# Three buffers for the first weights, the fourth one lent to a weight conversion, and one raw load per group moved forward

## The chip, the cores and the metric

The kernel runs on one core of a Trainium2 chip. The metric is the time of one execution on the device, in microseconds (us). TensorE (PE) multiplies matrices from SBUF into PSUM; VectorE (DVE) and ScalarE (ACT) work element by element; GpSimd (POOL) here does little but issue adding transfers; SyncE (SP) does nothing but issue the other transfers, one after the other: a transfer that has to wait for something holds up those behind it.

## The reference, cut to what matters

Windowed attention gives `x` (1152 tokens of 512), which goes through a mixture of four experts and then through one layer with a rational function:

```python
p = domain_probs / (domain_probs.sum(-1, keepdims=True) + 1e-09)
for e in range(E):                       # 4 experts, w1[e] 512x1024, w2[e] 1024x512
    h = np.maximum(x @ w1[e], 0.0)
    out += p[:, e:e + 1] * (h @ w2[e])
...
h = x @ w_in                             # 512x2048, given in float64
g = (a[0] + a[1]*h + a[2]*h*h + a[3]*h*h*h) / (1 + |b[0]|*|h| + |b[1]|*h*h + 1e-6)
return (g @ w_out).astype(np.float32)    # 2048x512, given in float64
```

## The kernel before, in words

**Split operands.** Every operand of a large product is kept as two parts: a rounded high part (made by an ACT copy) and the rest (made by a DVE subtraction). A product is three multiplications: high by high, high by low, low by high.

**Stages.** First comes attention, with the first group's products between its steps. Then come the groups of the expert layer. The expert layer's 4096 hidden columns are cut into 16 units `u` of 256, two to a group `g` (0 to 7), so there are 16 tiles `w1[u]` and 16 tiles `w2[u]`. The last stage treats the rational layer's 2048 columns as units 16 to 23, in an order written out by hand (`DENSE`).

**A group, g = 2 to 6.** On PE it has two plain first products (`h_paced`, L452: `ps_h<-xh,w`) for a third of the tokens, two calls of `strassen` (L904 and on), which make the other two thirds with seven products of blocks and of sums of blocks (L920: `ps_h<-...`), and nine second products (`o_paced`, L497: `ps_o<-w,hh` and `ps_o<-w,hl`). Inside `strassen` two DVE additions stand between PE's own products: PE cannot begin the next product before ACT has copied the fifth product to `p5` (L942) and DVE has added it (L943), and again later (L927). `relu_parts` makes the hidden operand's parts from a finished product: `hh` on ACT (L469), `hl` on DVE (L473). A second product needs both.

**Raw weights.** `load_w1` and `load_w2` (L139) load a unit's float32 tile (512 KB) into one of four `raw` buffers. `split_later` then copies it to the high half of a `w` tile (ACT, L815) and subtracts for the low half (DVE, L819). A `w1` tile also gets its block sums (L157) and those are split to `sw` (L840, L845). There are four `w` tiles of 8 KB a partition for `w1` and four for `w2`.

**The conversion.** While the groups run, `convert` turns the rational layer's float64 weights into float32 parts and stores them in DRAM. It works on half tiles: a load `x64` (L220, 512 KB, two buffers), some DVE steps (L242, L252, L269, L273, L283, L296) and one on ACT (L255) that give `f`, an ACT copy `high_part` (L225) and a DVE subtraction `low_part` (L229) into **one** split buffer `w` of 4 KB a partition, and a store of that buffer to DRAM (L230, 512 KB). The next `high_part` must wait until that store has landed. For six units (18 to 23) it also makes block sums in a buffer `sums` taken from the four `raw` ones, copies their high part into the same split buffer (L279), stores it (L280), subtracts (L286) and stores `sums` (L287).

**What sets the order.** `Pace` lays the steps of DVE and ACT between PE's products by a table of costs (`COST`), so the order on each engine is fixed when the program is built. `Window.open` says when the conversion may begin a unit with sums, and `Window.loaded` with the test `late` puts off the copy of the sums when raw loads have just been issued. `weights_free` runs when the first sums of a group are split, and issues the group's raw loads: `w1[u+3]`, `w2[u+2]`, `w2[u+3]`. The last one waits (`Window.waiting`) until the sums in work are stored.

Of the kernel before, what the change touches and what calls it, by code (L numbers as in the profile page):

```python
# [94 lines left out]
"""  # L95
COST = dict(h=2.09, p=1.045, o=2.74, osum=0.78, relu=1.0, add=0.59, split=0.67, sums=0.42, bits=0.41, both=1.15, token=1.0)
QSCALE = 1.0 / D ** 0.5
# [4 lines left out]
def body(ctx, tc, qkv, mask, dp, w1, w2, w1d, w2d, coef, out):  # L102
# [4 lines left out]
    hp = ctx.enter_context(tc.tile_pool(name="hp", bufs=6))  # L107
    wp = ctx.enter_context(tc.tile_pool(name="wp", bufs=4))
    dram = ctx.enter_context(tc.tile_pool(name="dram", bufs=1, space=DRAM))
    rawp = ctx.enter_context(tc.tile_pool(name="rawp", bufs=4))  # L110
# [20 lines left out]
    w1s, w2s, scratch = {}, {}, {}  # L131

    def load_w(src, store, nm):
        def load(u, halves=(slice(0, 1024),)):
            if u < 2 * NG1:
                if halves[0].start == 0:
                    store[u] = rawp.tile([128, 1024], F32, tag="raw", name="raw")
                for s in halves:
                    nc.sync.dma_start(store[u][:, s], src[u][:, s])  # L139
            elif u < 2 * NG:  # L140
                store[u] = wp.tile([128, 2, 1024], F32R, tag=nm, name=nm)
                nc.sync.dma_start(store[u].bitcast(F32), scratch[nm, u])
        return load
# [16 lines left out]
    def split_w(store, nm):  # L160
        def split(u, halves=(0, 1)):
            if u >= 2 * NG1:
                return
            if halves[0] == 0:
                raws[nm, u] = store[u]
                store[u] = wp.tile([128, 2, 1024], F32R, tag=nm, name=nm)
            raw, w = raws[nm, u], store[u]
            for i in halves:
                s = slice(i * 512, (i + 1) * 512)

                early = nm == "w1" and u < 2
                (nc.vector.tensor_copy if early else nc.scalar.copy)(w[:, 0, s], raw[:, s])
                nc.vector.tensor_tensor(
                    out=w[:, 1, s], in0=raw[:, s], in1=w[:, 0, s].bitcast(F32), op=ALU.subtract
                )
        return split
# [12 lines left out]
    class Window:  # L189

        open, loaded = False, -99.0
        waiting = []

    def convert(pool):
# [8 lines left out]
        def begin():  # L203
# [17 lines left out]
            return (nm, u, i), s, x, whole  # L221

        def high_part(f):
            w = pool.tile([128, 2, 512], F32R, tag="w", name="w")
            nc.scalar.copy(w[:, 0], f)  # L225
            return w
# [8 lines left out]
        while nxt or done:  # L235
# [29 lines left out]
            if x is not None:  # L265
# [9 lines left out]
                )  # L275
            late = x is None or Pace.pe - Window.loaded > 6.0
            if whole is not None and late:
                ws = pool.tile([128, 2, 512], F32R, tag="w", name="w").rearrange("p a b -> p (a b)")
                nc.scalar.copy(ws, whole)  # L279
                nc.sync.dma_start(scratch["sw", u][:, 0], ws.bitcast(F32))  # L280
            if x is not None:
                yield COST["split"]
                nc.vector.tensor_tensor(out=f, in0=f, in1=t.bitcast(F32), op=ALU.add)  # L283
            if whole is not None and late:
                yield COST["both"]
# [321 lines left out]
    with tc.manual_schedule():  # L607
# [53 lines left out]
        def split_high(n, u, i):  # L661
            store, nm = raw_of[n][1], f"w{n}"
            if i == 0:
                raws[nm, u] = store[u]
                store[u] = wp.tile([128, 2, 1024], F32R, tag=nm, name=nm)
            s = slice(i * 512, (i + 1) * 512)
            nc.scalar.copy(store[u][:, 0, s], raws[nm, u][:, s])
# [135 lines left out]
        def split_later(store, nm, u, wait=0.0):  # L803
            opens = nm == "w2" and u % 2 == 0

            def new(i):
                if i == 0:
                    raws[nm, u] = store[u]
                    store[u] = wp.tile([128, 2, 1024], F32R, tag=nm, name=nm)
            for i in range(2):  # L810
# [12 lines left out]
                def last(low=low):  # L823
                    low()
                    Window.open = True
                behind(0.0, (nm, u), act_then((nm, u), act, last if opens and i else low, COST["split"]), wait)

# [142 lines left out]
        def weights_free(*us):  # L970
            Window.open, Window.loaded = False, Pace.pe
            loads(*us)

        for g in range(NG1):
# [19 lines left out]
            if g in BLOCKED:  # L994
# [15 lines left out]
                w2_loads = (load_w2, u + 2), (load_w2, u + 3)  # L1010
                free = [(weights_free, *([(load_w1, u + 3)] if g > 1 else []), *(w2_loads if again else ()))]
                fills[2].insert(0, (sums_split_later, u + 1, 0, free))
# [6 lines left out]
                else:  # L1019
                    loads((load_w1, u + 4))  # L1020
                strassen(u + 1, (o((g, 0)), o((g, 1)), o((g, 2) if again else (g - 1, 8))))
                if again:
                    sums_split_later(u + 2, 0, [(loads, (load_w1, u + 4))])
                    sums_later(u + 3)
                else:
                    loads(*w2_loads, (load_w1, u + 5))

# [265 lines left out]
```

## Time and profile before

| what | value |
|---|---|
| three runs | 635.31, 637.47, 637.83 us; median 637.47 us |
| the profiled execution | 638.02 us, of which the span of the profile is 636.2 us |
| PE busy | 624.5 us (98%), 3726 matmuls |
| weight loads on PE | 556.7 us (88%) |
| DVE busy | 522.4 us (82%) |
| ACT busy | 369.2 us (58%) |
| POOL busy | 87.7 us (14%) |
| transfers | 111.28 MB, mean 175 GB/s |

The profiled execution is 0.55 us above the median and 1.8 us above its own span (what lies before the first and behind the last instruction). A wait is listed as the engine and line that waited, what ended the wait, the total, the times and the longest. The chain of waits follows the work that ended last back from the end. In the timeline the idle time ahead of an instruction stands in brackets. Names stand without their numbers: `x` is `x64`, `p` is `p5`, and `w<-w` is a store of a split buffer or a load of stored weights. SPq is SyncE issuing a transfer; a row of its timeline begins when it issues, not when the data has landed.

### The profile page before, as it was taken

How to read it: one execution, taken by the hardware profiler on the slowest of the kernel's cores; microseconds unless marked ns; L12 is line 12 of the kernel's file. 1: busy time of each engine (PE TensorE's matmuls, PEld its weight loads, DVE VectorE, ACT ScalarE, POOL GpSimd, SP SyncE). 2: the span in 40 equal slices, each digit the busy share in tenths (PEclk: the TensorE clock that was granted, in tenths of full speed). 3: DMA queues.
4: the chain of work that ended last, by engine and by line, in shares of the span. 5: the costliest groups of instructions: out<-in, count | busy, mean ns of one | idle time of the engine just before them, and what ended most of it. 6: DMA issues, size and time to landing. Idle time of an engine off the chain costs nothing.

```text
span 636.2 us, 9843 instructions
## 1 busy us (share of the span) xinstructions
PE 624.5 (98%) x3726; PEld 556.7 (88%) x3728; DVE 522.4 (82%) x788; ACT 369.2 (58%) x682; POOL 87.7 (14%) x103
## 2 busy tenths in 40 slices
PE   8999999999999999999999989999999999999997
PEld 4888898988989989899999978988998889899886
DVE  7687488889888888888879688438898899899994
ACT  6787624354554655454554454227688687877760
POOL 2223330011111111112111201000000002111110
PEclk9999999999999999999999989999999999999999
DMA  9955302259889778959778967870331563572333
GB/s 277 316 157 167 116 1 67 100 163 247 225 239 248 225 210 251 276 168 254 222 205 231 270 194 194 262 267 8 125 133 36 184 211 94 116 239 50 67 80 102
DMA packets 39535, 111.28 MB, mean 175 GB/s; under 512 B 4256, under 2 KB 5024, under 8 KB 37440
## 3 DMA queue, kind: packets, MB, share of 16 engines
q1 hardware_dynamic: 29264, 92.41, 43.6%
q0 software_dynamic: 9936, 18.09, 16.4%
q8 instruction: 29, 0.48, 0.3%
q10 hardware_dynamic: 288, 0.16, 0.1%
q14 instruction: 18, 0.15, 0.1%
HBM read 67.13 MB, written 25.43 MB: 145 GB/s over the span
## 4 chain that ended last, share of the span: by engine, by line
PE 91%; DMA 4%; DVE 3%; ACT 1%; issue 0%; POOL 0%; ACTq 0%; POOLq 0%
PE ps_o L497 42%; PE ps_h L452 21%; PE ps_h L920 14%; PE ps_h L1149 7%; DMA w<-w 3%; PE ps_v L416 2%; PE ps_s L402 1%; DMA raw<-in_w_dram 1%; PE ps_h L497 1%; PE ps_s L347 1%; PE ps_h L639 1%; PE ps_h L1083 1%; DVE hl L473 0%; DVE w L229 0%; DVE w L819 0%
## 5 line engine op out<-in xcount | busy, mean ns | idle before, releaser
L497 PE MATMUL ps_o<-w,hh 128*128 128x512 f32 (+1 forms) x848 | 229.6, 392 | 1.3 <-ACT hh L469 1.0
L497 PEld LDWEIGHTS ps_o<-w,hh 128*128 128x128 f32 x848 | 156.5, 188 | 29.7 <-ACT hh L469 1.5
L452 PE MATMUL ps_h<-xh,w 128*128 128x384 f32 x512 | 138.8, 339 | 0.0
L497 PE MATMUL ps_o<-w,hl 128*128 128x512 f32 (+1 forms) x424 | 132.0, 393 | 1.8 <-DVE hl L473 1.7
L497 PEld LDWEIGHTS ps_o<-w,hl 128*128 128x128 f32 x424 | 79.4, 188 | 20.0 <-DVE hl L473 2.7
L452 PEld LDWEIGHTS ps_h<-xh,w 128*128 128x128 f32 x512 | 93.9, 189 | 1.7 <-issue 0.3
L452 PE MATMUL ps_h<-xl,w 128*128 128x384 f32 x256 | 86.1, 336 | 0.0
L528 POOL DMA_DIRECT2D acc<-part x51 | 44.6, 875 | 282.0 <-ACT part L527 225.9
L527 ACT ACTIVATE part<-ps_o,p_sb 128x512 f32<-128x512 f32 x51 | 35.0, 686 | 59.1 <-PE ps_o L497 40.7
L469 ACT ACTIVATE hh<-ps_h 128x768 fp32r<-128x768 f32 x48 | 37.4, 810 | 31.3 <-PE ps_h L452 21.1
L473 DVE SCALAR_TENSOR_TENSOR hl<-ps_h,hh 128x768 fp32r<-128x768 f32 x48 | 44.5, 951 | 9.6 <-ACT hh L469 9.4
L452 PEld LDWEIGHTS ps_h<-xl,w 128*128 128x128 f32 x256 | 48.4, 189 | 0.8
L1068 POOL DMA_DIRECT2D acc<-part x18 | 15.6, 867 | 184.3 <-ACT part L1067 183.8
L920 PE MATMUL ps_h<-t,sw 128*128 128x384 f32 x168 | 34.4, 340 | 1.4 <-DVE ps_h L943 1.4
L819 DVE TENSOR_TENSOR w<-raw,w 128x512 fp32r<-128x512 f32 x48 | 32.9, 685 | 1.6 <-ACT w L815 1.5
L920 PEld LDWEIGHTS ps_h<-t,sw 128*128 128x128 f32 x168 | 30.2, 188 | 3.9 <-DVE ps_h L943 1.8
L381 ACT ACTIVATE pr<-pr,mx 128x80 f32<-128x80 f32 (+1 forms) x84 | 29.8, 358 | 6.1 <-DVE mx L375 4.7
L920 PE MATMUL ps_h<-xh,sw 128*128 128x384 f32 x112 | 33.2, 337 | 0.0
L920 PE MATMUL ps_h<-xh,w 128*128 128x384 f32 x112 | 33.1, 335 | 0.0
L564 DVE SCALAR_TENSOR_TENSOR sq<-sq,absb,ab 128x768 f32<-128x768 f32 x24 | 24.3, 1014 | 8.0 <-ACT sq L553 6.7
L815 ACT CAST w<-raw 128x512 fp32r<-128x512 f32 x48 | 28.1, 616 | 4.1 <-DMA raw<-in_w_dram 4.1
L255 ACT ACTIVATE x<-x 128x512 f32<-128x512 f32 x32 | 21.8, 681 | 13.7 <-DVE t L252 9.1
(133 smaller groups left out, 1082.7 us busy)
## 6 DMA issues: line engine op xcount, KB each, us to landing
acc<-part POOLq DMA_DIRECT2D x69, 256.0 KB, 3.9
raw<-in_w_dram SPq DMA_DIRECT2D x32, 512.0 KB, 6.1
w<-w SPq DMA_DIRECT2D x32, 512.0 KB, 3.7
w<-w SPq DMA_DIRECT2D x16, 1024.0 KB, 6.0
x<-in_w1d_dram SPq DMA_DIRECT2D x16, 512.0 KB, 4.2
x<-in_w2d_dram SPq DMA_DIRECT2D x16, 512.0 KB, 4.9
sw<-sw SPq DMA_DIRECT2D x12, 512.0 KB, 7.2
sw<-w SPq DMA_DIRECT2D x6, 512.0 KB, 2.7
```

The lines of the kernel that those rows point to most:

```text
L381: nc.scalar.activation(pr[:, j, i], pr[:, j, i], AF.Exp, scale=-1.0, bias=self.mx[:, j, i:i + 1], accum_out=self.total[:, j, i:i + 1],)
L452: nc.tensor.matmul(ps[:, i, :TC], lhsT=a[:, k, f], rhs=b[:, k], start=k + n == 0, stop=k + n == 5,)
L469: nc.scalar.activation(new_h(u, c)[0], ps[:, :, :TC], AF.Relu)
L473: nc.vector.scalar_tensor_tensor(out=hl, in0=ps[:, :, :TC], scalar=0.0, in1=hh.bitcast(F32), op0=ALU.max, op1=ALU.subtract,)
L497: nc.tensor.matmul(ps, lhsT=a[:, i, tk], rhs=b[:, i, cols], start=v + n == 0, stop=v + n == 6)
L527: nc.scalar.activation(part, ps, AF.Copy, scale=pe)
L528: nc.gpsimd.dma_start(acc[t], part, accum_op=ALU.add)
L564: nc.vector.scalar_tensor_tensor(out=self.sq, in0=self.sq, scalar=absb[:, 1:2], in1=self.ab, op0=ALU.mult, op1=ALU.add,)
L815: nc.scalar.copy(store[u][:, 0, s_], raws[nm, u][:, s_])
L819: nc.vector.tensor_tensor(out=w[:, 1, s_], in0=raws[nm, u][:, s_], in1=w[:, 0, s_].bitcast(F32), op=ALU.subtract)
L920: nc.tensor.matmul(out, lhsT=a[i][:, k], rhs=b[j][:, k], start=first and k + n == 0, stop=k + n == 3, skip_group_check=not first,)
L1149: nc.tensor.matmul(out, lhsT=a[i][:, k], rhs=b[j][:, k], start=first and k + m == 0, stop=k + m == 3, skip_group_check=not first,)
```

## The change

1. `w1` gets three buffers in place of four. A new single tile `lone` of the same size stands in for the fourth: it holds `w1[3]` early on, and `w1[19]` and `w1[23]` at the end (`weight_tile`).
2. Between those uses the two halves of `lone` are lent to the conversion as two more split buffers. `split_buffer` takes the pool's own buffer, `lone[:, 0]` and `lone[:, 1]` in turn, for `high_part` and for the copy of the sums.
3. One raw load per group moves forward: `w2[u+2]` is issued when the second half of the odd `w2` tile before it has been split (early in the group), not with the other raw loads in `weights_free`.
4. The test `late` and `Window.loaded` go: the copy of the sums is made as soon as the sums are there.
5. In the last group `w1[17]`, `w1[18]` and `w1[19]` are loaded one step later each.
6. `COST["split"]` goes from 0.67 to 0.68, so that the table lays DVE's and ACT's steps a little differently.

```diff
-COST = dict(..., split=0.67, ...)
+COST = dict(..., split=0.68, ...)
...
+    lone = ctx.enter_context(tc.tile_pool(name="lone", bufs=1)).tile([128, 2, 1024], F32R, name="lone")
...
+    def weight_tile(nm, u):
+
+        if nm == "w1" and (u == 3 or u >= 2 * NG1 and u % 4 == 3):
+            return lone
+        return wp.tile([128, 2, 1024], F32R, tag=nm, name=nm, bufs=3 if nm == "w1" else 4)
...
-                store[u] = wp.tile([128, 2, 1024], F32R, tag=nm, name=nm)
+                store[u] = weight_tile(nm, u)
...
+        def split_buffer():
+            Window.spare.append(Window.spare.pop(0) if Window.spare else None)
+            own = pool.tile([128, 1024], F32R, tag="w", name="w") if Window.spare[-1] is None else None
+            return own if own is not None else Window.spare[-1]
+
         def high_part(f):
-            w = pool.tile([128, 2, 512], F32R, tag="w", name="w")
+            w = split_buffer().rearrange("p (i n) -> p i n", i=2)
             nc.scalar.copy(w[:, 0], f)
             return w
...
-            late = x is None or Pace.pe - Window.loaded > 6.0
-            if whole is not None and late:
-                ws = pool.tile([128, 2, 512], F32R, tag="w", name="w").rearrange("p a b -> p (a b)")
+            if whole is not None:
+                ws = split_buffer()
                 nc.scalar.copy(ws, whole)
                 nc.sync.dma_start(scratch["sw", u][:, 0], ws.bitcast(F32))
...
                 def last(low=low):
                     low()
-                    Window.open = True
+                    if u % 2 == 0:
+                        Window.open = True
+                    elif u + 1 < 2 * NG1:
+                        load_w2(u + 1)
...
                 w2_loads = (load_w2, u + 2), (load_w2, u + 3)
-                free = [(weights_free, *([(load_w1, u + 3)] if g > 1 else []), *(w2_loads if again else ()))]
+                free = [(load_w1, u + 3)] * (g > 1) + [w2_loads[0]] * (g == 1) + [w2_loads[1]]
+                free = [(weights_free, *free)] if again else []
...
-                    loads((load_w1, u + 4))
+                    loads((load_w1, u + 3))
                 strassen(u + 1, (o((g, 0)), o((g, 1)), o((g, 2) if again else (g - 1, 8))))
+                if g == 1:
+                    Window.spare[:] = [None, lone[:, 0], lone[:, 1]]
...
-                    loads(*w2_loads, (load_w1, u + 5))
+                    loads(*w2_loads, (load_w1, u + 4), (load_w1, u + 5))
```

**The order on PE** is the same in both programs, row by row, apart from the name of the tile. The order of DVE, ACT and SP changes from the second group on. Line numbers of the changed file are 10 to 16 higher (L139 becomes L146, L220 L228, L230 L243, L287 L299, L819 L829, L943 L956).

SP's queue in group 4 before, from the store of the sums of unit 20 on. `raw_2790` is `w1[11]`, `raw_2792` and `raw_2794` are `w2[10]` and `w2[11]`, `x64` are loads of the conversion:

```order
L280 DMA sw_20_1394<-w_2772 128x1024
L287 DMA sw_20_1394<-sums_2486 128x1024
L139 DMA raw_2790<-in_w1_dram 128x1024
L139 DMA raw_2792<-in_w2_dram 128x1024
L139 DMA raw_2794<-in_w2_dram 128x1024
L220 DMA x64_2803<-in_w2d_dram 128x1024
L230 DMA w2_18_1380<-w_2821 256x1x512
```

The same place now, with what stands ahead of it; `raw_2635` is `w2[10]`, `raw_2769` `w1[11]`, `raw_2806` `w2[11]`:

```order
L146 DMA raw_2635<-in_w2_dram 128x1024
L243 DMA w2_18_1383<-lone_73 256x1x512
L228 DMA x64_2677<-in_w2d_dram 128x1024
L243 DMA w1_20_1391<-lone_73 256x1x512
L228 DMA x64_2721<-in_w2d_dram 128x1024
L243 DMA w1_20_1391<-w_2734 256x1x512
L146 DMA raw_2769<-in_w1_dram 128x1024
L292 DMA sw_20_1397<-lone_73 128x1024
L299 DMA sw_20_1397<-sums_2507 128x1024
L146 DMA raw_2806<-in_w2_dram 128x1024
L228 DMA x64_2840<-in_w2d_dram 128x1024
L243 DMA w2_18_1383<-lone_73 256x1x512
```

The load of `w2[10]` moved ahead of three stores, two `x64` loads, the load of `w1[11]` and both stores of the sums. The load of `w2[11]` still stands right behind the store of the sums, and it takes the buffer that this store frees, in groups 3 to 6 alike. Three buffers take turns where one did.

SP's queue in group 6 before (`raw_3687` is `w1[15]`, `raw_3689` and `raw_3709` are `w2[14]` and `w2[15]`):

```order
L280 DMA sw_22_1396<-w_3683 128x1024
L139 DMA raw_3687<-in_w1_dram 128x1024
L139 DMA raw_3689<-in_w2_dram 128x1024
L287 DMA sw_22_1396<-sums_3402 128x1024
L139 DMA raw_3709<-in_w2_dram 128x1024
L220 DMA x64_3712<-in_w2d_dram 128x1024
L230 DMA w2_22_1384<-w_3767 256x1x512
```

And now (`raw_3670` is `w1[15]`, `raw_3672` `w2[15]`; `w2[14]` is loaded five rows ahead of this piece):

```order
L292 DMA sw_22_1399<-lone_73 128x1024
L299 DMA sw_22_1399<-sums_3356 128x1024
L146 DMA raw_3670<-in_w1_dram 128x1024
L146 DMA raw_3672<-in_w2_dram 128x1024
L228 DMA x64_3681<-in_w2d_dram 128x1024
L243 DMA w2_21_1386<-lone_73 256x1x512
```

Two raw loads stood between the two stores of the sums; none does now.

DVE's queue in group 3 of the changed kernel. The row ahead of these, `L308 ... f_2277<-x64_2192`, frees the buffer into which `x64_2332` is loaded; that load stands on SP behind the store of the sums and two raw loads, as above:

```order
L255 TENSOR_SCALAR t_2334<-x64_2242 128x512
L265 SCALAR_TENSOR_TENSOR t_2334<-x64_2242,t_2334 128x512
L242 TENSOR_TENSOR lone_73<-f_2277,lone_73 128x512
L282 TENSOR_SCALAR f_2347<-t_2334 128x512
L164 TENSOR_TENSOR raw_2081<-raw_2081 128x2x128
L485 SCALAR_TENSOR_TENSOR hl_2349<-ps_h_2201,hh_2348 128x768
L485 SCALAR_TENSOR_TENSOR hl_2352<-ps_h_2202,hh_2351 128x768
L164 TENSOR_TENSOR raw_2081<-raw_2081 128x2x128 x3
L286 SCALAR_TENSOR_TENSOR f_2347<-x64_2242,f_2347 128x512
L295 TENSOR_TENSOR f_2347<-f_2347,t_2334 128x512
L858 TENSOR_TENSOR sw_2392<-raw_2081,sw_2392 128x512
L956 TENSOR_TENSOR ps_h_2355<-ps_h_2354,p5_2402 128x384
```

Behind them come `L308 ... f_2347<-x64_2242` and `L829 ... w2_2418`, and then `L255 ... t_2424<-x64_2332`, the first use of the new load. That is 16 instructions between the two uses of the buffer; in groups 4, 5 and 6 it is 14, 18 and 18.

## Rows read from the trace of the kernel before

**Rows 1.** The page's first part: busy time, share of the span, instructions.
```profile
PE 624.5 (98%) x3726; PEld 556.7 (88%) x3728; DVE 522.4 (82%) x788; ACT 369.2 (58%) x682; POOL 87.7 (14%) x103
```
**Rows 2.** Table by stretches: length, five engines' busy time, PEclk, DMA share, GB/s.
```profile
182.86:230.76 47.90, 47.90 (x242) 43.35 (x241) 42.50 (x75) 25.20 (x42) 7.80 (x9) 1.00 0.82 235
230.76:280.32 49.56, 48.16 (x241) 43.27 (x241) 42.77 (x74) 26.30 (x44) 7.86 (x9) 1.00 0.81 230
```
**Rows 3.** Waits of PE from 78 to 430 us, the longest three.
```profile
PE ps_o L497 <- DVE hl L473: 1.7, 1, 1.7
PE ps_h L920 <- DVE ps_h L943: 1.4, 1, 1.4
PE ps_o L497 <- ACT hh L469: 1.0, 1, 1.0
```
**Rows 4.** The chain of waits from 228 to 264 us: start, length, what.
```profile
227.98 2.77 PE ps_h L452 x16
...
239.59 4.48 DMA w<-w
...
245.52 3.65 DMA w<-w
...
252.53 7.76 DMA raw<-in_w_dram
...
261.35 0.58 DVE ps_h L943
```
**Rows 5.** PE's timeline from 355 to 392 us, at the longest wait.
```profile
374.46 1.22 PE L497 MATMUL ps_o<-w,hl 128*128 128x512 f32 x2 [1.69 <-DVE hl L473]
```
**Rows 6.** Table by stretches again: the four microseconds behind that wait.
```profile
374.00:378.00 4.00, 3.54 (x12) 3.35 (x13) 3.93 (x9) 1.71 (x3) 0.56 (x1) 0.57 0.55 195
```
**Rows 7.** SP's timeline from 345 to 372 us: start of issue, length, line.
```profile
348.92 0.33 SPq L280 DMA_DIRECT2D sw<-w  x1
349.29 1.26 SPq L139 DMA_DIRECT2D raw<-in_w_dram  x2
350.65 0.41 SPq L287 DMA_DIRECT2D sw<-sums  x1
358.89 0.33 SPq L139 DMA_DIRECT2D raw<-in_w_dram  x1
359.31 0.41 SPq L220 DMA_DIRECT2D x<-in_w2d_dram  x1
359.81 1.08 SPq L230 DMA_DIRECT2D w<-w  x1
```
**Rows 8.** DVE's timeline from 361 to 376 us.
```profile
366.18 0.43 DVE L242 TENSOR_SCALAR t<-x 128x512 uint32<-128x512 uint32 x1 [4.25 <-DMA x<-in_w2d_dram]
...
369.59 0.69 DVE L229 TENSOR_TENSOR w<-f,w 128x512 fp32r<-128x512 f32 x1 [1.79 <-ACT w L225]
...
372.59 1.81 DVE L473 SCALAR_TENSOR_TENSOR hl<-ps_h,hh 128x768 fp32r<-128x768 f32 x2
...
374.92 1.34 DVE L157 TENSOR_TENSOR raw<-raw 128x256 f32<-128x256 f32 x3
```
**Rows 9.** The chain of waits from 355 to 386 us, at the same place.
```profile
359.81 9.03 DMA w<-w
```
**Rows 10.** Waits of ACT from 86.86 to 410 us, one of them.
```profile
ACT w L225 <- DMA w<-w: 20.1, 8, 5.3
```
**Rows 11.** Transfers of one line to landing: line 287 (`sums` stores).
```profile
DMA to landing us min/median/max: 3.2/3.5/8.2
```
**Rows 12.** The same for line 220 (`x64` loads).
```profile
DMA to landing us min/median/max: 3.2/4.4/9.6
```
**Rows 13.** The page's part 6: transfers by line, count, KB, median us to landing.
```profile
raw<-in_w_dram SPq DMA_DIRECT2D x32, 512.0 KB, 6.1
w<-w SPq DMA_DIRECT2D x32, 512.0 KB, 3.7
w<-w SPq DMA_DIRECT2D x16, 1024.0 KB, 6.0
```

More of the change, by code (lines that the diff above doesn't have):

```diff
@@ L95 @@
 """
-COST = dict(h=2.09, p=1.045, o=2.74, osum=0.78, relu=1.0, add=0.59, split=0.67, sums=0.42, bits=0.41, both=1.15, token=1.0)
+COST = dict(h=2.09, p=1.045, o=2.74, osum=0.78, relu=1.0, add=0.59, split=0.68, sums=0.42, bits=0.41, both=1.15, token=1.0)
 QSCALE = 1.0 / D ** 0.5
@@ L165, in split @@
                 raws[nm, u] = store[u]
-                store[u] = wp.tile([128, 2, 1024], F32R, tag=nm, name=nm)
+                store[u] = weight_tile(nm, u)
             raw, w = raws[nm, u], store[u]
@@ L189, in body @@
     class Window:
-        open, loaded = False, -99.0
+        open = False
         waiting = []
+        spare = []
     def convert(pool):
@@ L283, in convert @@
                 nc.vector.tensor_tensor(out=f, in0=f, in1=t.bitcast(F32), op=ALU.add)
-            if whole is not None and late:
+            if whole is not None:
                 yield COST["both"]
@@ L664, in split_high @@
                 raws[nm, u] = store[u]
-                store[u] = wp.tile([128, 2, 1024], F32R, tag=nm, name=nm)
+                store[u] = weight_tile(nm, u)
             s = slice(i * 512, (i + 1) * 512)
@@ L803, in split_later @@
         def split_later(store, nm, u, wait=0.0):
-            opens = nm == "w2" and u % 2 == 0
             def new(i):
@@ L808, in new @@
                     raws[nm, u] = store[u]
-                    store[u] = wp.tile([128, 2, 1024], F32R, tag=nm, name=nm)
+                    store[u] = weight_tile(nm, u)
             for i in range(2):
@@ L824, in last @@
                     low()
-                    Window.open = True
-                behind(0.0, (nm, u), act_then((nm, u), act, last if opens and i else low, COST["split"]), wait)
+                    if u % 2 == 0:
+                        Window.open = True
+                    elif u + 1 < 2 * NG1:
+                        load_w2(u + 1)
+                behind(0.0, (nm, u), act_then((nm, u), act, last if nm == "w2" and i else low, COST["split"]), wait)
         sw = {}
@@ L970, in weights_free @@
         def weights_free(*us):
-            Window.open, Window.loaded = False, Pace.pe
+            Window.open = False
             loads(*us)
```

## The prediction

> **What bounds the kernel now.** The page's first part comes first: PE is busy 98% of the span, DVE 82%, ACT 58% [rows 1]. So PE's own work is the floor, and only what lets PE stand still or run slowly can be won. PE's order and work do not change, so the next question is where PE loses time in the stretch that the change touches, the groups from 87 to 430 us.
>
> The table by stretches answers it. An undisturbed group lasts 47.90 us and PE is busy for all of it. The next one lasts 49.56 us [rows 2]: 1.66 us lost. PE's waits name the places: 1.4 us for the DVE addition L943, which is the loss in that group, and 1.0 us for `hh` and 1.7 us for `hl` right after each other [rows 3], at 371 to 374 us [rows 5]. Behind this last pair the granted clock falls: over 374 to 378 us it is 0.57 of full speed [rows 6], so part of that stretch ran at 1.2 GHz instead of 2.4. That costs 4 x (1 - 0.57) = 1.72 us more. In all
>
> 1.66 + 1.0 + 1.7 + 1.72 = 6.1 us, 1.0% of the span.
>
> This is the most the change can win in the groups.
>
> Why PE waited is read from the chain of waits. Ahead of the first loss it goes twice through the store of the split buffer, 4.48 and 3.65 us, then through the load of a raw weight tile, 7.76 us, and ends in L943 [rows 4]. DVE ran late because ACT could not refill the only split buffer; being late, it freed a raw buffer late; the raw load that waited for it came late; and ACT, which works in order, stood before the `w2` copy with the copy to `p5` behind it.
>
> Ahead of the second loss SP's queue was held. It issued two raw loads and the store of the sums at 349 to 351 us, and then nothing until 358.89, because the next raw load needed the buffer that this store frees [rows 7]: 8.24 us. The conversion's load and its store, queued behind, went out at 359.31 and 359.81. DVE waited 4.25 us for that load and 1.79 us for ACT, 6.0 us together [rows 8], and ACT was waiting for the store, which took 9.03 us to land [rows 9]. DVE's `hl` came at 372.6 [rows 8], and PE stood.
>
> **The change part by part.**
>
> *Two more split buffers.* Waits of ACT for the one buffer sum to 20.1 us in eight places, up to 5.3 us [rows 10]. With three buffers in turn a refill needs the store of three uses earlier. A half tile takes DVE seven operations (L242, L252, L269, L273, L283, L296, L229) of 0.43 to 0.69 us [rows 8], some 4 us, so three uses lie about 12 us apart. A store lands in 3.7 us in the median [rows 13] and took 9.03 at its worst place [rows 9]. So these waits go. Nothing replaces them on DVE: the number of operations is the same. The gain on PE is between 0 (all cover elsewhere) and 6.1 us.
>
> *The raw load moved forward.* In group 4 `w2[u+2]` was issued at 252.53 us and landed 7.76 us later, with the path to L943 waiting for it [rows 4]. Three stores and two `x64` loads of the conversion lie between its new place and the old, three half tiles at some 4 us, so it goes out about 12 us earlier or more. That is seven times the 1.66 us by which it was late; this closes the first loss even where a store is slow. What it passes are stores and `x64` loads: each stands behind 512 KB more for one transfer's time. Between nothing and 3 us per passed transfer (9.03 us for the last of three issued together, [rows 7, 9]), and covered because the loads it passes are used many operations later. I take 0.
>
> *The load of `w2[u+3]`* stays right behind the store of the sums and still waits for its landing, so SP is still held once in each of groups 3 to 6. What changes is how long. In group 6 two raw loads and a store were queued ahead of the store of the sums, and it took 8.24 us; in the changed order only the other store of the sums is, or one raw load more in group 4. The median landing is 3.5 us, the worst 8.2 [rows 11]. Group 3 is tightest: between freeing the `x64` buffer and its next use stand 16 operations. By the rows: 1.81 us for the two `hl`, 1.34 and a third of it for the four raw sums, two narrow ones at 0.43, seven at up to 0.69 [rows 8] and the addition at 0.58 [rows 4], 9.9 us. The store of the sums goes out about 1.4 us (two operations) before the buffer is free; SP is held to 3.5 - 1.4 = 2.1 us after; the load then lands 4.4 us later in the median, 9.0 behind two raw loads [rows 12, 9]. So 6.5 to 11.1 us against 9.9: DVE waits 0 to 1.2 us. Since 6.0 us of such waits gave PE 2.7 us of waiting [rows 8, 3], the first 3.3 us reach nobody. I take 0; the upper end, with a store of 8.2 us, is a rival below.
>
> By the Trainium skill, "DMA: Bandwidth & Descriptors", section "Queues, rings and completion order", each DMA engine consumes the descriptors of a ring in order. By that rule a load that is pulled forward delays what stands behind it by its full length, the store of the sums and `x64` too, and the sum would be that of the slower rival below. The trace agrees where three transfers went out together in group 6: the third landed last. It does not agree that this is the usual case: the median `x64` load lands in half of that time.
>
> *Three `w1` buffers.* A new `w1` tile now waits for the unit three before instead of four. ACT's copy for `w1[u+3]` stands behind the `hh` copies that wait for the last product of `strassen(u)`, the same product that frees the buffer. It waits for nothing new. If that cover went, it would be one product of six matmuls, 2.77 x 6/16 = 1.04 us [rows 4].
>
> *The last loads.* `w1[18]` and `w1[19]` go out behind `w2[16]` and `w2[17]`. 1 MB takes 6.0 us [rows 13]; four of them 24 us. The first product with `w1[18]` stands behind twelve bank steps of twelve matmuls in `DENSE`, 12 x 12 x 2.77/16 = 25 us by the same row, and behind the second products between them. 0.
>
> *Dropping `late`, 0.68 for 0.67.* These shift the order by an operation or two; the additions that PE waits for keep their place between the same products. I put 0.5 us on this and on all else that is new, between 0 and the 1.66 us of one loss like the first.
>
> **The sum** against the profiled execution: 638.02 - 6.1 + 0.5 = 632.4 us. That execution is 0.55 us above the median of the runs, so against the median: 637.47 - 5.6 = **631.9 us**.
>
> **The rivals.** What a measurement of this kernel can tell from no change is 0.5%, 3.2 us: below 634.3 is faster, above 640.7 slower.
>
> *One loss stays.* For: the losses come once in some six groups, so small shifts make and unmake them. If one like the first stays: 631.9 + 1.66 = 633.6, still faster. If one like the second stays, clock and all (2.7 + 1.72 = 4.4): 636.3, no change. The second is for the reader who distrusts the step on SP: the queue is held as before, only behind fewer bytes.
>
> *The buffers are not what binds.* ACT works in order, and its split copies often stand behind a copy that waits for PE. Then DVE's wait for ACT stays with any number of buffers: 637.5. Against it: the waits of ACT at L225 name the store [rows 10].
>
> *SP's hold becomes the bound: slower.* The store of the sums lands late (8.2 us) in each group, since the pulled-forward load and the undelayed copy of the sums bunch the transfers; `x64` comes 4.7 us later than above, 11.2 to 15.8 us after its buffer is free. DVE then waits up to 5.9 us in group 3. It decides from 3.3 us of DVE waiting in a group; each group beyond that costs what the second loss cost, 4.4 us. Three groups: 637.47 - 6.1 + 3 x 4.4 = 644.6 us. Two give 640.2, which is no change yet. Against it: half of the six stores of sums landed in 3.5 us or less [rows 11], and groups 5 and 6 have 18 operations for cover. (The Trainium skill's rule on ring order, above, is this rival's.)
>
> **How the numbers follow.** Both losses go: 0.70 (631.9). One like the first stays: 0.08 (633.6). One like the second stays: 0.10 (636.3). The buffers do not bind: 0.07 (637.5). SP's hold: 0.05 (644.6). Faster 0.70 + 0.08 = 0.78, no change 0.17, slower 0.05. The range goes from 630.0, the forecast less its 0.5 and less 1.4 for runs that spread from 635.31 to 637.83, to 636.5, which takes in one loss like the second and leaves out 0.12 and a little of the rest.
>
> **What would show it.** Right: no wait of PE over 0.3 us from 130 to 415 us, granted clock 1.00 all through, every group 47.9 us; ACT's waits for stores at the split copies near 0; SP still held for about 3 us once in groups 3 to 6. A step is wrong if DVE waits for `x64` for over 3.3 us in a group, if ACT still waits for a store of a split buffer, or if PE waits at L956 (the old L943). The forecast is wrong if PE's waits in the groups sum to over 2 us or if the clock falls once.

## The result, and the profile after

The changed kernel takes **631.46 us** in the median of 6 runs (631.32 to 632.67), the kernel before 637.60 us in the median of 6 (635.31 to 640.90). The ratio is 0.9908, with a 95% interval from 0.9880 to 0.9936: faster by about 0.9%. Forecast were 631.9 us and a range from 630.0 to 636.5. The runs also lie closer together: 1.35 us from lowest to highest, against 5.6 us.

The page's first part of the changed kernel answers to [rows 1]; PE is now busy 99% of a span of 629.6 us (before: 636.2).

```profile
PE 622.5 (99%) x3726; PEld 556.3 (88%) x3728; DVE 522.9 (83%) x788; ACT 370.2 (59%) x682; POOL 87.7 (14%) x103
```

These are all waits of PE that the whole span holds (total, times, longest). The three of [rows 3] are gone, and none of these four lies in the groups: they are two places at PE's start, one of the attention and one second product at 77.7 us, ahead of the stretch that the change touches.

```profile
PE ps_h L651 <- DVE warm L641: 1.2, 1, 1.2
PE ps_s L414 <- POOL pr L403: 0.7, 1, 0.7
PE ps_h L651 <- issue: 0.3, 1, 0.3
PE ps_o L509 <- DVE xl L452: 0.3, 1, 0.3
```

The table by stretches answers to [rows 2, 6]: every group from 135 us on lasts 47.90 us, PE is busy for all of each, and the granted clock is 1.00.

```profile
182.86:230.76 47.90, 47.90 (x242) 43.38 (x241) 41.15 (x71) 25.17 (x43) 7.81 (x9) 1.00 0.81 227
230.76:278.65 47.89, 47.89 (x242) 43.36 (x241) 42.54 (x74) 25.10 (x43) 7.82 (x9) 1.00 0.84 232
326.55:374.44 47.89, 47.89 (x242) 43.36 (x241) 40.56 (x70) 25.43 (x43) 7.82 (x9) 1.00 0.85 238
374.44:414.00 39.56, 39.56 (x200) 35.21 (x199) 27.55 (x45) 15.65 (x25) 4.43 (x5) 1.00 0.75 229
```

In the table of ACT's waits the row of 20.1 us for the split buffer's store [rows 10] has no successor. What the split copies (L238, L291) still wait for is DVE. The only wait for a transfer is the one for `acc`, in two places.

```profile
ACT lone L291 <- DVE sums L164: 2.8, 2, 2.3
ACT w L238 <- DVE f L308: 2.0, 1, 2.0
...
ACT part L539 <- DMA acc<-part: 4.7, 2, 3.2
```

SP is still held behind each store of the sums: 3.5 us in group 3, 5.5 in group 4, where one raw load more goes out ahead of the two stores, 3.2 in group 5 and 3.3 in group 6. Its timeline in group 6 answers to [rows 7]: the store is issued at 346.03 and the load that it holds at 349.32 us, 3.3 us later in place of 8.24. (The row of two raw loads spans the hold: the second waits.)

```profile
342.33 0.33 SPq L292 DMA_DIRECT2D sw<-lone  x1
346.03 0.33 SPq L299 DMA_DIRECT2D sw<-sums  x1
346.63 3.02 SPq L146 DMA_DIRECT2D raw<-in_w_dram  x2
349.75 0.46 SPq L228 DMA_DIRECT2D x<-in_w2d_dram  x1
```

The tightest place is in group 3. There the `x64` load went out at 205.06 us, and DVE waited 0.55 us for it, as DVE's timeline shows (the one wait of this kind before was 4.25 us, ahead of group 7, [rows 8]):

```profile
212.44 0.43 DVE L255 TENSOR_SCALAR t<-x 128x512 uint32<-128x512 uint32 x1 [0.55 <-DMA x<-in_w2d_dram]
```

So the time went where the forecast looked for it. By PE's timeline the same second products begin 0.33 us earlier than before in group 3 (182.37 for 182.70), 2.01 us earlier in group 5 (278.15 for 280.16) and 6.64 us earlier in group 7 (373.94 for 380.58), and that lead stays to the end. So the first loss gave back 1.7 us and the second 4.6, its waits and the low clock together. The other 0.3 us lie at the start, in a stretch that the change does not touch.

### The profile page after: what moved, and what is told of

The parts are those of the page before. It is cut to its first block, busy times and chain, and to the rows that moved or that the text cites. A ratio compares the mean times of both kernels' runs of the same rounds, so it can differ in the third digit from the quotient of the medians.

```text
span 629.6 us, 9848 instructions
## 1 busy us (share of the span) xinstructions
PE 622.5 (99%) x3726; PEld 556.3 (88%) x3728; DVE 522.9 (83%) x788; ACT 370.2 (59%) x682; POOL 87.7 (14%) x103
## 4 chain that ended last, share of the span: by engine, by line
PE 97%; DVE 1%; ACT 0%; POOL 0%; issue 0%; POOLq 0%
PE ps_o L509 46%; PE ps_h L464 21%; PE ps_h L933 16%; PE ps_h L1165 7%; PE ps_v L428 2%; PE ps_s L414 1%; PE ps_h L509 1%; PE ps_s L359 1%; PE ps_h L651 1%; PE ps_h L1099 1%; DVE mx L387 0%; DVE pr L377 0%; POOL pr L403 0%; PE ps L359 0%; DVE xl L889 0%; DVE hl L485 0%
## 5 line engine op out<-in xcount | busy, mean ns | idle before, releaser
L464 PE MATMUL ps_h<-xh,w 128*128 128x384 f32 x464 | 125.3, 338 | 0.0
L464 PEld LDWEIGHTS ps_h<-xh,w 128*128 128x128 f32 x464 | 84.4, 188 | 1.3
L464 PE MATMUL ps_h<-xl,w 128*128 128x384 f32 x232 | 77.7, 335 | 0.0
L464 PEld LDWEIGHTS ps_h<-xl,w 128*128 128x128 f32 x232 | 43.6, 188 | 0.6
L829 DVE TENSOR_TENSOR w<-raw,w 128x512 fp32r<-128x512 f32 x48 | 32.8, 684 | 1.0 <-ACT w L825 0.9
L933 PE MATMUL ps_h<-xh,w 128*128 128x384 f32 x104 | 30.7, 336 | 0.0
L825 ACT CAST w<-raw 128x512 fp32r<-128x512 f32 x48 | 27.9, 616 | 0.0
```

Source lines behind the costliest of these rows:

```text
L464: nc.tensor.matmul(ps[:, i, :TC], lhsT=a[:, k, f], rhs=b[:, k], start=k + n == 0, stop=k + n == 5,)
L825: nc.scalar.copy(store[u][:, 0, s_], raws[nm, u][:, s_])
L829: nc.vector.tensor_tensor(out=w[:, 1, s_], in0=raws[nm, u][:, s_], in1=w[:, 0, s_].bitcast(F32), op=ALU.subtract)
L933: nc.tensor.matmul(out, lhsT=a[i][:, k], rhs=b[j][:, k], start=first and k + n == 0, stop=k + n == 3, skip_group_check=not first,)
```

## The experiments

The question is which part of the change did it. The forecast gave the second loss (4.4 us) to the two further split buffers and the first (1.66 us) to the moved raw load, and it held the shift of the order for nothing. All kernels below were timed in 5 rounds, in three sets on three chips, each ratio against runs of the kernel before on the same chip. Those had medians of 638.81 us (11 runs) beside the kernel with one buffer, the two with the raw load put back and the one with the buffers in the old order; 638.65 us (17 runs) beside the one with two buffers and the three with the raw load, the price or `late` changed alone; and 638.61 us (29 runs, 634.71 to 641.27) beside the four on the hold of SP, the third set. Line numbers differ by a few from kernel to kernel.

**One part taken from the change.** First the two further split buffers:

```diff
-                if g == 1:
-                    Window.spare[:] = [None, lone[:, 0], lone[:, 1]]
```

> The changed kernel with one split buffer instead of three (the lent fourth weight buffer stands idle); order of every engine and the moved raw load as changed. Theory (one buffer makes DVE late): ACT's waits for stores of the split buffer come back, 15 to 25 us in sum in the groups, some half tile ends late enough for PE, and one loss like the second of before returns: 633.0 to 637.5 us, PE waits of 1 to 3 us in the groups and a stretch with the clock below 1.00. Rival A (the moved raw load and the new order did it): ACT's waits come back but no PE wait over 0.5 us, 631.0 to 632.3 us.

Measured: 633.37 us (632.70 to 634.58), ratio to before 0.9913 [0.9886, 0.9940]. The theory holds in its time, at the lower end, and in the kind of wait: some 1.9 us come back, not 6. ACT waits for the stores again, 27.9 us in two rows (15 to 25 were expected). PE has one loss, like the first of before but at another place, 197.95 us, and the low clock that was expected does not come:

```profile
ACT w L238 <- DMA w<-w: 16.8, 8, 3.9
...
ACT w L291 <- DMA w<-w: 11.1, 4, 3.6
```
```profile
PE ps_h L933 <- DVE ps_h L956: 1.4, 1, 1.4
```

Then one of the two further buffers (`[None, lone[:, 0]]`):

> The changed kernel with two split buffers instead of three. With one it took 633.37 us, with three 631.46. Theory (a refill needs the store of two uses earlier, some 8 us, and stores land in about 4 and at worst 9): ACT's waits for stores fall from 28 us to 1 to 6 us, PE waits below 1 us in the groups, 631.4 to 632.2 us. Rival (the third buffer is needed, because three stores in a row go out together when a tile's sums are done): 632.5 to 633.5 us.

Measured: 631.76 us (631.25 to 632.61), 0.9904 [0.9883, 0.9925]. No wait of ACT for a split store, where 1 to 6 us were expected, and no wait of PE in the groups. The third buffer is not needed.

Then the moved raw load, put back:

```diff
-                    elif u + 1 < 2 * NG1:
-                        load_w2(u + 1)
...
-                free = [(load_w1, u + 3)] * (g > 1) + [w2_loads[0]] * (g == 1) + [w2_loads[1]]
+                free = [(load_w1, u + 3)] * (g > 1) + [*w2_loads]
```

> The changed kernel with the load of w2[u+2] put back to where it was, right ahead of w2[u+3] behind the store of the sums, in groups 4 to 6; three split buffers and order of DVE, ACT and PE as changed. Theory (the late raw load was a loss of its own, 1.66 us): ACT waits for the w2 load in at least one group and PE 0.5 to 2 us behind it, 632.0 to 633.5 us. Rival A (the raw load was late only since DVE was late, which three buffers mend): 631.2 to 631.8 us, PE's waits in the groups below 0.3 us. Rival B (SP's hold grows by a load and becomes the bound): DVE waits over 3.3 us for x64, 634 us or more.

Measured: 631.74 us (630.88 to 632.05), 0.9883 [0.9859, 0.9907]. Rival A holds in its time: the load, back among the group's raw loads, was not late in group 4. SP's timeline has it as the second of two there, issued at 250.65 us (before: 252.53, [rows 4]), and ACT's timeline has the copy that needs it without a wait:

```profile
247.88 3.10 SPq L146 DMA_DIRECT2D raw<-in_w_dram  x2
```
```profile
257.23 0.62 ACT L825 CAST w<-raw 128x512 fp32r<-128x512 f32 x1
```

It does not stand where it stood before, though: in this order both stores of the sums go out behind it (251.88 and 253.14 us), where they went out ahead of it. At two later places ACT waits 0.63 and 0.56 us for a raw load, and no wait of PE follows. So this run alone does not tell the buffers from the order; the old order with three buffers, below, does.

**Both taken.** One split buffer and the raw load in its old place; what stays is the order by 0.68 and without `late`, and three buffers for `w1`.

> The changed kernel with one split buffer and the raw load not moved: what is left of the change in the groups is the order of DVE and ACT (0.68, no test for lateness) and three buffers for w1. Theory (the order is worth nothing; the buffers and the load are): 635.0 to 639.0 us, one or two losses as before. Rival (a shift of the order by an operation or two already unmakes the losses, the buffers and the load are idle): 631.2 to 632.5 us.

Measured: 633.49 us (632.53 to 634.66), 0.9911 [0.9886, 0.9937]. Neither theory: most of the gain stays, but not all. PE waits 1.8 us in three places, none of which is a place of before, and the clock stays at 1.00. With one buffer the raw load is worth nothing in this order (633.37 with it, 633.49 without).

**One part added to the kernel before.** The buffers alone: three split buffers, with the three `w1` buffers that make room for them; 0.67 and `late` as before, raw load in its old place.

> The order of before (0.67, lateness test) and the raw load not moved, with three w1 buffers, the lent buffer and so three split buffers. Theory (the buffers close the second loss, 4.4 us, and by half or all the first, 1.66 us): 631.5 to 633.6 us, no wait of ACT for a store of a split buffer. Rival (the order did it): 636 to 638 us, with PE waiting 1 to 3 us for DVE in the groups though ACT waits for no store.

Measured: 631.83 us (631.57 to 632.12), 0.9886 [0.9862, 0.9910]. The buffers alone do all of it in the old order too. Here the raw load was still late once, in group 4, and it cost PE 0.2 us in place of 1.4; the waits of ACT and of PE in the groups:

```profile
ACT w L826 <- DMA raw<-in_w_dram: 2.1, 1, 2.1
```
```profile
PE ps_h L931 <- DVE ps_h L954: 0.2, 1, 0.2
```

In group 6 SP was held as long as before, 8.60 us (347.53 to 356.13) behind the same two raw loads, and DVE waited 2.26 us for `x64`. It waited for no split buffer, and PE waited for nothing there:

```profile
347.53 0.33 SPq L300 DMA_DIRECT2D sw<-sums  x1
356.13 0.33 SPq L146 DMA_DIRECT2D raw<-in_w_dram  x1
```
```profile
362.40 0.43 DVE L255 TENSOR_SCALAR t<-x 128x512 uint32<-128x512 uint32 x1 [2.26 <-DMA x<-in_w2d_dram]
```

So the long hold alone does not make the second loss.

The moved raw load alone; DVE, ACT and PE keep the order of before word for word, only SP's changes:

> The kernel before with the load of w2[u+2] moved forward, and nothing else: one split buffer, order of DVE and ACT as before. Theory (the raw load follows from DVE's lateness and is no loss of its own; the single buffer is): 635.5 to 639 us, ACT's waits for stores stay near 20 us, and PE still stands before hl or an addition in the groups. Rival (the late raw load made the first loss, 1.66 us of it): 1.0 to 2.0 us below the before of the same chip, with no wait of ACT for a w2 raw load.

Measured: 633.42 us (632.20 to 634.58), 0.9930 [0.9908, 0.9952]. This is below what either theory allowed. ACT waits for the stores as before (18.2 and 13.2 us), yet both losses are gone. The first went as the rival says: ACT waits for no raw load in the groups (before: 4.1 us at two places), and PE does not wait in group 4. It has one wait of 0.7 us, at 396.88. For the loss at group 7 SP's timeline shows what changed: one raw load instead of two stands ahead of the store of the sums, SP is held 5.3 us instead of 8.24, and the `x64` load goes out at 353.33 instead of 359.31 [rows 7].

```profile
346.76 0.42 SPq L139 DMA_DIRECT2D raw<-in_w_dram  x1
347.64 0.37 SPq L287 DMA_DIRECT2D sw<-sums  x1
352.91 0.33 SPq L139 DMA_DIRECT2D raw<-in_w_dram  x1
353.33 0.45 SPq L220 DMA_DIRECT2D x<-in_w2d_dram  x1
```

DVE's timeline has no wait for that load. It still waits 1.95 us for ACT and the one buffer, but `hl` is done 6 us earlier than in [rows 8], ahead of PE:

```profile
363.37 0.69 DVE L229 TENSOR_TENSOR w<-f,w 128x512 fp32r<-128x512 f32 x1 [1.95 <-ACT w L225]
...
366.37 1.81 DVE L473 SCALAR_TENSOR_TENSOR hl<-ps_h,hh 128x768 fp32r<-128x768 f32 x2
```

The price of a split alone (`split=0.68` in the kernel before):

> The kernel before with the planner's price of a split at 0.68 instead of 0.67, and nothing else. It shifts the order of DVE and ACT. The new order with one buffer took 633.49 us, and this run shows how much of that is the price. Theory (the losses come where a late half tile happens to meet an addition or hl that PE waits for; any shift moves them): anywhere from 632.5 to 639 us, with ACT's waits for stores still 15 to 30 us in sum and PE's waits at other places than before. Rival (it is the lateness test that made the loss at group 7): 636.5 to 639 us, with PE waiting 1 us and more at 371 to 374 us as before.

Measured: 632.89 us (631.79 to 633.28), 0.9915 [0.9892, 0.9938]. The theory's wide range holds, the rival falls: a hundredth of a microsecond in the planner's price is worth some 5 us, though ACT waits as long as before (19.2 and 15.4 us). PE waits at another place, 165.29 us, and the clock stays up:

```profile
165.29 1.34 PE L920 MATMUL ps_h<-t,sw 128*128 128x384 f32 x6 [1.27 <-DVE ps_h L943]
```

At group 7, where the loss is gone, SP's timeline shows a short hold: in the new order the store of the sums goes out ahead of all three raw loads of group 6, the third is held 3.2 us behind it (issued at 352.15), and `x64` follows at 352.57 in place of 359.31 [rows 7].

```profile
348.90 0.33 SPq L287 DMA_DIRECT2D sw<-sums  x1
349.27 3.20 SPq L139 DMA_DIRECT2D raw<-in_w_dram  x3
```

The test `late` taken from the kernel before, and nothing else:

> The kernel before without the test for lateness (a finished tile's sums are split at once, always), price of a split 0.67, one buffer, loads as before. Theory (any shift moves the losses): 632.5 to 639 us, waits of ACT for stores 15 to 30 us, PE's waits elsewhere than before. Rival (the test held stores back until they bunched with two raw loads ahead of group 7, the 8.24 us hold; without it the hold is half as long): 632.5 to 634 us, no clock below 1.00 in the groups, SP's longest hold below 6 us.

Measured: 636.84 us (633.88 to 638.63), 0.9967 [0.9945, 0.9990]. The theory's wide range holds, the rival does not: the loss at group 7 is gone, but four others stand in its place:

```profile
PE ps_h L919 <- DVE ps_h L942: 3.4, 3, 1.4
PE ps_o L496 <- DVE hl L472: 1.1, 1, 1.1
```

The wait for `hl` is the loss of group 7 again, one group earlier and smaller. SP is held 8.15 us behind a store of the sums (303.13 to 311.28, where the rival put the longest hold below 6). Then DVE waits for `x64` and for ACT, which waits 3.32 us for the store of the one buffer, and PE stands before `hl`; SP's, DVE's and PE's timelines:

```profile
303.13 0.40 SPq L286 DMA_DIRECT2D sw<-sums  x1
311.28 0.33 SPq L139 DMA_DIRECT2D raw<-in_w_dram  x1
```
```profile
317.52 0.43 DVE L242 TENSOR_SCALAR t<-x 128x512 uint32<-128x512 uint32 x1 [2.29 <-DMA x<-in_w2d_dram]
...
320.94 0.69 DVE L229 TENSOR_TENSOR w<-f,w 128x512 fp32r<-128x512 f32 x1 [1.80 <-ACT w L225]
```
```profile
325.82 0.74 PE L496 MATMUL ps_o<-w,hl 128*128 128x512 f32 x2 [1.05 <-DVE hl L472]
```

Together these waits of DVE are 4.1 us, against 6.0 before [rows 8], and the clock stays up.

**The hold of SP.** The kernel before, with the load that holds SP issued behind the conversion's next load and store; DVE, ACT and PE keep their order.

```diff
-                while Window.waiting:
-                    Window.waiting.pop(0)()
+                Window.ready.extend(Window.waiting)
+                Window.waiting.clear()
...
             stored.add(key)
+            while Window.ready:
+                Window.ready.pop(0)()
```

> The kernel before with the load of w2[u+3] issued behind the conversion's next load and store on SP, instead of ahead of them, wherever it waited for the store of the sums; order of DVE, ACT and PE unchanged, one split buffer. Theory (the loss at group 7 needs both: the 8.24 us hold of SP, by which the x64 load and the split store go out late, and the one buffer that must wait for that store): the hold is lifted, DVE waits for x64 below 1 us, the waits at 371 to 374 us and the low clock go: 632.5 to 634.5 us. Rival (the buffer alone makes that loss): 636.5 to 639.5 us, waits of PE there as before.

Measured: 639.91 us (637.45 to 644.00), 1.0028 [1.0004, 1.0051]: a miss, and the rival falls too. The part on the loss at group 7 came out: PE has no wait at 371 to 374 us, and the clock stays at 1.00. But the raw load, now behind, is late itself. In group 3 it goes out at 181.18 us instead of 172.07, as the chain shows; ACT waits 5.90 us for it (its timeline) and hands the delay to DVE and PE.

```profile
181.18 5.13 DMA raw<-in_w_dram
```
```profile
186.33 1.14 ACT L817 CAST w<-raw 128x512 fp32r<-128x512 f32 x2 [5.90 <-DMA raw<-in_w_dram]
```

PE's waits in the groups sum to 6.6 us:

```profile
PE ps_h L922 <- DVE ps_h L945: 4.0, 3, 1.7
PE ps_h L922 <- ACT ps_h L936: 2.6, 2, 1.7
```

The other three kernels make the hold longer, by stores of the same sums to a place that nobody reads (n = 1 or 3):

```diff
+                for k in range(n):
+                    nc.sync.dma_start(scratch["more", k], whole)
                 nc.sync.dma_start(scratch["sw", u][:, 1], whole)
```

> The changed kernel with one further store of 512 KB of the same sums ahead of the store that w2[u+3] waits for, so that SP is held longer, by one transfer's time, 1.5 to 4 us, once in each of groups 3 to 6. It adds only traffic. Theory (the first 3.3 us of DVE's wait for x64 reach nobody, with three buffers): DVE's waits for x64 grow to 1 to 3 us a group, PE still waits below 0.5 us in the groups, 631.3 to 632.5 us. Rival (there is no such cover left, the hold is the bound now): PE waits 1 us or more, 633 us or more.

Measured: 631.78 us (631.29 to 632.74), 0.9904 [0.9878, 0.9930]. The theory holds for the time and for PE: `x64` went out 2.0 us later in group 3 (207.08 for 205.06), DVE waited 1.62 us, PE nothing. In groups 4 to 6 DVE waited for no `x64`, where 1 to 3 us were expected.

> The changed kernel with three further stores of sums, so that SP is held 5 to 10 us longer once in each of groups 3 to 6. Theory (DVE's wait for x64 goes over 3.3 us in a group, and what is above it reaches PE): DVE waits 3 to 8 us for x64 in two groups or more, PE 1 to 3 us in the worst of them, 633 to 642 us. Rival (the two x64 buffers and the lead that DVE has cover even this): below 632.5 us.

Measured: 635.01 us (633.37 to 636.68), 0.9955 [0.9934, 0.9977]. The theory holds. SP's timeline in group 3: `x64` goes out at 210.94 us, 5.9 us later than in the changed kernel.

```profile
200.85 1.69 SPq L303 DMA_DIRECT2D more<-sums  x3
202.58 1.18 SPq L304 DMA_DIRECT2D sw<-sums  x1
203.86 6.99 SPq L146 DMA_DIRECT2D raw<-in_w_dram  x2
210.94 0.42 SPq L231 DMA_DIRECT2D x<-in_w2d_dram  x1
```

DVE's timeline at that place and at two later ones, and PE's behind the first and the third: a wait of 3.33 us reaches nobody, one of 5.83 us costs PE 2.19 us. In group 6 even a wait of 1.53 us is followed by one of PE, 0.64 us, one addition later: the cover is not the same everywhere.

```profile
217.40 0.43 DVE L258 TENSOR_SCALAR t<-x 128x512 uint32<-128x512 uint32 x1 [5.83 <-DMA x<-in_w2d_dram]
...
319.06 0.43 DVE L258 TENSOR_SCALAR t<-x 128x512 uint32<-128x512 uint32 x1 [3.33 <-DMA x<-in_w2d_dram]
...
343.04 0.43 DVE L258 TENSOR_SCALAR t<-x 128x512 uint32<-128x512 uint32 x1 [1.53 <-DMA x<-in_w2d_dram]
```
```profile
219.08 0.44 PE L938 MATMUL ps_h<-xh,sw 128*128 128x384 f32 x1 [2.19 <-DVE ps_h L945]
...
344.72 1.31 PE L938 MATMUL ps_h<-t,sw 128*128 128x384 f32 x6 [0.64 <-DVE ps_h L961]
```

> The same further store of sums, with one split buffer instead of three (without it: 633.37 us). Theory (a longer hold and one buffer add up on DVE: the split store behind the hold is late, and ACT needs it): 634.5 to 638.5 us, PE waits of 2 us and more in the groups. Rival (they do not add; the one buffer alone sets what is lost): 633.0 to 634.2 us.

Measured: 634.55 us (632.94 to 637.62), 0.9933 [0.9912, 0.9953]. The theory holds, at its lower end: the store that costs 0.3 us in the median with three buffers costs 1.2 us with one (633.37 to 634.55). In the profiled run (637.62, the longest of its 12) DVE waits 2.14 us for ACT, and PE stands for the addition behind it:

```profile
196.90 0.69 DVE L245 TENSOR_TENSOR w<-sums,w 128x512 fp32r<-128x512 f32 x1 [2.14 <-ACT w L241]
```
```profile
198.58 1.31 PE L938 MATMUL ps_h<-t,sw 128*128 128x384 f32 x6 [1.82 <-DVE ps_h L961]
```

## Why the prediction was right, point by point

The time and the floor came out as forecast, and the two further split buffers do what was said of them. What was wrong is how the gain was shared out among the parts of the change. In one table, by number of split buffers:

| split buffers | rest of the kernel | us, median |
|---|---|---|
| 3 | as changed | 631.46 |
| 3 | raw load not moved | 631.74 |
| 3 | old order, raw load not moved | 631.83 |
| 3 | as changed, one further store in the hold | 631.78 |
| 2 | as changed | 631.76 |
| 3 | as changed, three further stores in the hold | 635.01 |
| 1 | before, 0.68 alone | 632.89 |
| 1 | as changed | 633.37 |
| 1 | before, raw load moved | 633.42 |
| 1 | as changed, raw load not moved | 633.49 |
| 1 | as changed, one further store in the hold | 634.55 |
| 1 | before, no `late` | 636.84 |
| 1 | before (beside the third set) | 638.61 |
| 1 | before, raw load behind `x64` | 639.91 |

- **The most that could be won, 6.1 us.** Right: PE is busy for the whole of every group now, and PE's products show 6.3 us from the two losses. It fits that no kernel here has a median below the changed one's: nothing of PE's waiting is left in the groups.
- **Two more split buffers.** Right in mechanism and sign. With two or three, ACT's waits for stores go, and all five such kernels but the one with three further stores lie from 631.5 to 631.8 us, whatever else they have. The buffers are the only part of the change that removes all the losses by itself.
- **The raw load closes the first loss.** Right that it does: moved alone, in the order of before, it leaves ACT no wait for a raw load and PE none in group 4. Wrong that it is the part that is needed for it. With three buffers in the old order the load may stay where it was: ACT still waits 2.1 us for it, but PE only 0.2. And moved alone it also removes the second loss, which the forecast had given to the buffers, because SP's hold, with one raw load fewer ahead of it, is then 5.3 us.
- **The shift of the order, 0 to 1.66 us against the change.** This step failed, in sign and size: the price 0.68 alone takes off some 5 us, dropping `late` alone about 2 (ratio 0.9967). The sum came out right because these gains are not added: the buffers, the raw load and the price each remove the two losses, and what one has removed the next cannot. That the shares were wrong could not show in the sum; so far it was luck.
- **The hold of SP, taken as 0, and 3.3 us of cover on DVE.** Right for the hold, and for the cover in group 3: there 1.62 us of waiting for `x64` cost nothing and 5.83 us cost 2.19, so that the cover was some 3.6 us. It is no constant of the kernel: 3.33 us cost nothing at 319.06 us, but 1.53 us at 343.04 cost 0.64. The slower rival has the right mechanism and the wrong distance: it takes holds 6 us longer than the changed kernel's, and gives 635.0 us then. By the Trainium skill, "DMA: Bandwidth & Descriptors", section "Queues, rings and completion order", each DMA engine consumes the descriptors of a ring in order. The traces agree: with one store put ahead of the store of the sums `x64` went out 2.0 us later, with three 5.9. What the rule leaves open is whether anyone is waiting.
- **Three `w1` buffers, the last loads: 0.** Right: no wait of PE in the groups, and from 430 to 560 us PE is busy 129.91 us, as before (129.90).
- **0.5 us for the rest.** Not seen. The profiled execution is 6.67 us faster: 6.3 are the two losses, and 0.3 is PE's start, where kernels that share the code differ by more (34.80 to 37.04 us busy in the first 39).
- **One loss stays.** This rival is what the kernels with one buffer show: PE's waits in the groups of four of them (one buffer, one buffer with the raw load put back, the raw load alone, the price alone) sum to 0.7 to 1.8 us, with the clock at 1.00, at 632.9 to 633.5 us, much as the 633.6 us that the rival gave for a loss like the first.

What was shown: each edit that was put alone into the kernel before unmakes the loss at group 7, and the buffers unmake all losses but 0.2 us. That loss takes both the long hold of SP and the one split buffer. With the hold shortened or lifted and one buffer it is gone; with the hold at 8.60 us and three buffers it is gone too; and without `late`, with one buffer and a hold of 8.15 us, it came back one group earlier, at 1.05 us. The price alone unmakes it by shortening the hold to 3.2 us. Why the price and `late` make other waits in other groups was not taken apart.

## What to carry to other kernels

When a kernel's runs spread by 5 us and a price changed by a hundredth moves it by as much, judge an edit by the slack that it adds and not by its time alone: here a further store cost 0.3 us in the median with three split buffers and 1.2 with one. Gains that cover for one another are not added; take each part out of the change and put each alone into the kernel before. A long sum of waits on an engine beside the bound says little: kernels with 25.8 to 37.8 us of ACT's waits for split stores took from 633 to 640 us; what counts is whether one of them ends ahead of something that PE needs.

## What the runs showed of the hardware

The granted clock fell three times in the groups in these profiles, each time behind waits of PE, and each fall cost about the same. Before, it was behind 1.03 and 1.69 us in close succession (1.72 us lost, [rows 3, 6]). With one buffer and the longer hold it was behind 1.82 us, with the much longer hold behind 2.19 us; the table by stretches of these two, in this order, gives 6 x (1 - 0.72) = 1.7 us for each:

```profile
198.00:204.00 6.00, 5.42 (x20) 4.91 (x21) 4.96 (x11) 1.95 (x3) 0.86 (x1) 0.72 0.72 222
```
```profile
218.00:224.00 6.00, 4.92 (x19) 4.92 (x20) 5.93 (x11) 3.84 (x7) 0.86 (x1) 0.72 0.77 205
```

Each is a fall from 2.4 to 1.2 GHz. In the kernel with the raw load behind `x64`, waits of 1.70 us (twice) and 1.45 us left the clock at 1.00; what decides between the two outcomes these runs do not tell. Where it falls, it adds about 1.7 us to the wait.

The runs without a trace fit this. Of the 29 runs of the kernel before in the third set, the six from 634.71 to 636.57 us have a mean granted clock of 0.998 to 1.000, and the 13 from 639.07 us on 0.993 to 0.997; in between it is mixed. One fall of 1.7 us takes some 0.003 off the mean of 636 us. So part of that kernel's spread lies in the clock; where it fell in those runs no trace shows.
